# Down projection of a SwiGLU block: three of four quads in 32-row strips throughout

## The chip, the cores and the metric

The kernel runs on one core of one Trainium2 chip. TensorE does the matrix multiplications into eight PSUM banks, VectorE and ScalarE read the banks, SyncE issues most transfers. The metric is the device time of one execution in microseconds (us); the time of a version is the median of its runs. One execution is also profiled, and its span (from its first to its last instruction) is a little shorter than its time.

## What is computed

```
B, S, D, F = 1, 2048, 512, 1376
g = silu(x @ w_gate)
u = x @ w_up
out = (g * u) @ w_down
```

All inputs and the output are bf16. S is 2048 rows (tokens), D is 512, F is 1376, which is ten blocks of 128 and a remainder of 96.

## The kernel before

**Gate and up.** Tokens are split into four chunks of 512 columns (`SC`, `NSC`), each into four tiles of 128 tokens (`TPC`). For each chunk c and each of the ten whole blocks of F (`ft`), `plan_pair` plans a group G (gate) and a group U (up): four matmuls each over D, 512 columns wide. ScalarE applies silu to G, VectorE multiplies it with U and writes `hT_sb[:, ft, tokens]` (L280, L289). So `hT_sb` holds the hidden values with F on the partitions.

**The remainder of 96.** It is laid out in strips of 32 rows (`R`). Each chunk has an X group (`plan_x`): the last 96 gate columns and the last 32 up columns together. Two Y groups (`plan_y`) hold the other 64 up columns of two chunks each. VectorE's products of X and Y go to `ht_sb[32c:32c+32, q, :]`: chunk c lies on its own 32 partitions, with q = 0, 1, 2 (`NR`) counting the strips of the remainder. The two Y groups come last of all groups before the down projection. VectorE makes nine products of them: two for each chunk, and one for `hl_sb`, which the last output tile uses.

**Down projection.** There are 16 output tiles of 128 tokens x 512 columns. Each tile needs ten matmuls with 128 rows (`hT_sb` against `wd_sb`) and the remainder of 96 rows. Tiles are grouped into four quads: quad j holds tile j of each of the four chunks, so that the four tiles of a quad have their remainders on four different groups of 32 partitions. `whole_rows` (L394) does the ten 128-row matmuls of a tile. `tail_rows` (L408) does the remainder of a quad: three rounds (q) of four matmuls of 32 rows, each on another row group of TensorE's array, so that four can run side by side, and each into another bank.

The order is: quad 0 whole, quad 0 tail, quad 1 tail, quad 1 whole; then the same for quads 2 and 3. The last tile of quad 3 is split into columns 0 to 384 and 384 to 512; the narrow piece is the group `last`, and its remainder is one matmul with 96 rows (L431).

**Banks and waits.** Groups take the eight banks in turn (`add_group`), in the order in which they are planned: transposes, the four chunks with their X, the two Y, then the output groups in tile order. Thus a group's bank was last used by the group eight before it. `free(g)` makes TensorE wait until the readers of that earlier group are done. For quad 0 these are the eighth U group of the last chunk (counted from 1), the ninth G and U, and the tenth G; for quad 1 they are the last U, the last X and the two Y groups. `after` waits for a count on ScalarE's or VectorE's semaphore, and `need` for a load. TensorE's instructions run in program order.

**Copies and stores.** VectorE copies each finished output bank to one of three buffers `o_sb` (`NOS`; L293); ScalarE copies only the 384-wide piece of the last tile. SP issues the stores in tile order (L258), each after its copy, and waits at the end for all of them.

## Time and profile before

| what | us |
|---|---|
| median of 3 runs | 120.66 (120.31 to 120.93) |
| the profiled execution | 120.32 |
| its span | 118.9 |
| start of the down projection | 79.19 |
| first tail (quads 0 and 1), start | 87.93 |
| second tail (quads 2 and 3), start | 106.71 |
| last matmul, start | 116.78 |
| last store landed, end of the span | 118.9 |

Two more groups of the page, for later use (line, engine, operation, out<-in, shapes, count, then the busy time, the mean of one in ns, and the idle time of the engine before them with what ended it):

```profile
L394 PE MATMUL bank<-wd_sb,hT_sb 128*128 128x512 bf16 (+2 forms) x166 | 34.5, 366 | 0.4 <-issue 0.3
L293 DVE CAST o_sb<-bank 128x512 bf16<-128x512 f32 (+1 forms) x16 | 10.1, 663 | 22.0 <-PE bank L408 12.3
```

How to read them: PE is TensorE's matmuls, PEld its weight loads, DVE VectorE, ACT ScalarE, SP SyncE. Matmuls are pipelined: one of 379 ns starts before the one ahead of it has ended, so the pitch of starts and not the duration of one gives the rate. Some matmul records are missing from a trace: here about one in fifty, which is why 166 are listed where the program issues 170. In timelines the first column is the start in us and the second the time that the merged instructions cover.

### The profile page before, as it was taken

What the parts mean: (1) busy time and instruction counts of PE and PEld (TensorE: products, weight loads), DVE (VectorE), ACT (ScalarE), POOL (GpSimd) and SP (SyncE); (2) the same over time, 40 slices, a digit from 0 to 9 for tenths busy, and PEclk for the clock granted to TensorE, in tenths of its full rate; (3) what the DMA queues carried; (4) which work ended last, traced back from release to release, by engine and by line L of the source; (5) the groups of instructions that cost most, each with busy time, mean ns of one, the idle gap of its engine ahead of it and who ended that gap; (6) DMA issues with size and microseconds to landing.
All of it is one profiled execution on the core that took longest, in us unless ns stands there. A gap on an engine that the chain in (4) does not pass through costs nothing.

```text
span 118.9 us, 1519 instructions
## 1 busy us (share of the span) xinstructions
PE 115.4 (97%) x600; PEld 54.1 (45%) x611; DVE 47.3 (40%) x73; ACT 31.0 (26%) x53; POOL 0.4 (0%) x5
## 2 busy tenths in 40 slices
PE   7999999999999999999999999999999999999993
PEld 2774444444444444444444444344434444444452
DVE  0133443353443444433444334469617422006530
ACT  4344324454234363244262343230000000000001
POOL 1000000000000000000000000000000000000000
PEclk9999999999999999999999999999999999999999
DMA  3999999970000000000000000000004221002412
GB/s 103 271 307 357 264 162 242 328 183 24 0 0 0 6 0 0 0 3 3 0 0 0 6 0 0 0 0 0 0 0 138 88 88 44 0 0 75 145 50 88
DMA packets 17559, 8.84 MB, mean 74 GB/s; under 512 B 10640, under 2 KB 17424, under 8 KB 17552
## 3 DMA queue, kind: packets, MB, share of 16 engines
q1 hardware_dynamic: 16496, 8.48, 26.7%
q10 hardware_dynamic: 1056, 0.26, 1.0%
q8 instruction: 5, 0.08, 0.3%
q14 instruction: 2, 0.02, 0.1%
HBM read 4.81 MB, written 2.10 MB: 58 GB/s over the span
## 4 chain that ended last, share of the span: by engine, by line
PE 97%; issue 1%; DVE 0%
PE bank L328 58%; PE bank L394 29%; PE bank L370 3%; PE bank L337 2%; PE bank L408 2%; PE bank L381 2%; PE bank L346 1%; DVE o_sb L293 0%; PE bank L431 0%
## 5 line engine op out<-in xcount | busy, mean ns | idle before, releaser
L328 PE MATMUL bank<-xT_sb,w_sb 128*128 128x512 bf16 (+2 forms) x338 | 69.7, 364 | 0.4
L328 PEld LDWEIGHTS bank<-xT_sb,w_sb 128*128 128x128 bf16 x344 | 32.8, 98 | 36.4 <-issue 0.2
L289 DVE TENSOR_TENSOR hT_sb<-sg_sb,bank 128x512 bf16<-128x512 f32 x40 | 27.5, 688 | 40.5 <-PE bank L328 36.6
L394 PE MATMUL bank<-wd_sb,hT_sb 128*128 128x512 bf16 (+2 forms) x166 | 34.5, 366 | 0.4 <-issue 0.3
L280 ACT ACTIVATE sg_sb<-bank 128x512 f32<-128x512 f32 x40 | 23.8, 596 | 40.8 <-PE bank L328 40.8
L394 PEld LDWEIGHTS bank<-wd_sb,hT_sb 128*128 128x128 bf16 x170 | 16.1, 98 | 19.1 <-issue 1.3
L293 DVE CAST o_sb<-bank 128x512 bf16<-128x512 f32 (+1 forms) x16 | 10.1, 663 | 22.0 <-PE bank L408 12.3
L280 ACT ACTIVATE o_sb<-bank 128x384 bf16<-128x384 f32 x1 | 0.5, 492 | 37.8 <-PE bank L394 37.8
L289 DVE TENSOR_TENSOR ht_sb<-sgy_sb,bank 32x512 bf16<-32x512 f32 x8 | 5.5, 684 | 0.2
L289 DVE TENSOR_TENSOR ht_sb<-sgx_sb,bank 32x512 bf16<-32x512 f32 x4 | 2.8, 691 | 3.5 <-ACT sgx_sb L280 3.5
L370 PE MATMUL bank<-xT_sb,w_sb 128*128 128x512 bf16 x15 | 4.1, 379 | 0.1
L337 PE MATMUL bank<-const-bfloat16-1.0 128*128 128x512 bf16 (+1 forms) x8 | 2.9, 545 | 0.8 <-PEq L454 0.8
L280 ACT ACTIVATE sgx_sb<-bank 32x512 f32<-32x512 f32 x4 | 2.4, 588 | 4.5 <-PE bank L370 4.5
L408 PE MATMUL bank<-wdt_sb,ht_sb 32*128 32x512 bf16 (+1 forms) x48 | 2.9, 372 | 0.0
L370 PEld LDWEIGHTS bank<-xT_sb,w_sb 128*128 128x128 bf16 x16 | 1.6, 98 | 1.9
L280 ACT ACTIVATE sgy_sb<-bank 64x512 f32<-64x512 f32 x4 | 2.4, 590 | 0.1
L337 PEld LDWEIGHTS bank<-const-bfloat16-1.0 128*128 128x128 bf16 x8 | 1.0, 136 | 2.4 <-issue 2.4
L381 PE MATMUL bank<-xT_sb,w_sb 128*64 128x512 bf16 x16 | 1.9, 382 | 0.0
L408 PEld LDWEIGHTS bank<-wdt_sb,ht_sb 32*128 32x128 bf16 x48 | 1.1, 93 | 1.7 <-issue 0.8
L269 ACT ACT_TABLE_LOAD x1 | 1.3, 1283 | 1.8 <-issue 1.8
L293 DVE COPY xT_sb<-bank 128x256 bf16<-128x256 bf16 x2 | 0.6, 292 | 2.7 <-PE bank L346 2.7
L381 PEld LDWEIGHTS bank<-xT_sb,w_sb 128*64 128x64 bf16 x16 | 0.8, 109 | 1.0 <-DVE hT_sb L289 0.4
(14 smaller groups left out, 4.0 us busy)
## 6 DMA issues: line engine op xcount, KB each, us to landing
out_dram<-o_sb SPq DMA_DIRECT2D x15, 128.0 KB, 1.7
wd_sb<-in_w_down_dram SPq DMA_DIRECT2D x1, 1280.0 KB, 9.2
w_sb<-in_w_gate_dram SPq DMA_DIRECT2D x1, 480.0 KB, 5.9
w_sb<-in_w_up_dram SPq DMA_DIRECT2D x1, 448.0 KB, 6.5
w_sb<-in_w_gate_dram SPq DMA_DIRECT2D x1, 384.0 KB, 4.5
w_sb<-in_w_up_dram SPq DMA_DIRECT2D x1, 384.0 KB, 5.1
wdt_sb<-in_w_down_dram SPq DMA_DIRECT2D x4, 96.0 KB, 7.5
xn_sb<-in_x_dram SPq DMA_DIRECT2D x1, 256.0 KB, 2.8
```

The lines of the kernel that those rows point to most:

```text
L269: act.activation(adummy[:, 0:4], zero_c, ACT.Silu)
L280: act.activation(op["out"], op["src"], fn).then_inc(s_A, 1)
L289: ins = dve.tensor_tensor(op["out"], op["a"], op["b"], ALU.mult)
L293: ins = dve.tensor_copy(op["out"], op["src"])
L328: ins = pe.matmul(g["bank"][:, n0:n1], lhsT=w_sb[:, dk, col:col + P], rhs=xT_sb[:, dk, c * SC + n0:c * SC + n1], start=(dk == 0), stop=(dk ...
L337: pe.matmul(banks[NB - 1][:, 0:width], lhsT=ones_w, rhs=ones_m[:, 0:width], start=True, stop=True)
L346: ins = pe.transpose(tview(g["bank"])[:, k, :], xn_sb[:, g["i"], dk * P:(dk + 1) * P], ident[:, :])
L370: ins = pe.matmul(g["bank"][:, :], lhsT=w_sb[:, dk, XC0:XC0 + P], rhs=xT_sb[:, dk, c * SC:(c + 1) * SC], start=(dk == 0), stop=(dk == KD - 1),
L381: ins = pe.matmul(g["bank"][y0:y1, :], lhsT=w_sb[:, dk, YC0:YC0 + 64], rhs=xT_sb[:, dk, c * SC:(c + 1) * SC], start=(dk == 0), stop=(dk == ...
L394: ins = pe.matmul(g["bank"][:, 0:c1 - c0], lhsT=hT_sb[:, fk, t * P:(t + 1) * P], rhs=wd_sb[:, fk, c0:c1], start=(start and fk == 0), stop= ...
L408: ins = pe.matmul(g["bank"][:, 0:c1 - c0], lhsT=ht_sb[R * c:R * (c + 1), q, j * P:(j + 1) * P], rhs=wdt_sb[R * c:R * (c + 1), q, c0:c1], s ...
```

## The change

Quads 0, 1 and 2 (`qa`, `qb`, `qc`) are computed in strips of 32 rows: `whole_rows` remains for quad 3 (`qd`) and for the narrow piece of the last tile. A 128-row block of F is cut into four strips of 32 rows. In a round, the four tiles of a quad each run one strip of the same block, tile c on row group (c - turn) mod 4; after ten rounds (one per block of F) the turn goes up by one, so that after four turns each tile has had all four strips. [...]

The order is: ten rounds of `qa`, ten of `qb`, alternating through turns 0, 1, 2; turn 3 of `qa`; both tails (three rounds each); turn 3 of `qb`. Then `qc`: its tail and turn 0 (13 rounds), and before each of its turns 1, 2, 3 one round of `qd`'s tail. Then `qd` whole, and the narrow piece.

There are eight output buffers instead of three, and in the first three quads ScalarE makes the copies of the tiles with odd c.

```diff
-    NOS = 3
+    NOS = 8
...
-                eng = "A" if len(halves) == 2 and c0 == 0 else "D"
+                eng = "A" if (j < TPC - 1 and c % 2) or (len(halves) == 2 and c0 == 0) else "D"
...
-            for i in range(NOS):
-                sp.wait_ge(s_out[i], 16 * n_store[i])
+            for i in range(NST, NST + NOS):
+                sp.wait_ge(s_out[i % NOS], 16 * n_store[i % NOS])
...
             def whole_rows(g, start, stop):
-                free(g)
-                after("D", h_ready[g["c"]])
+                if start:
+                    free(g)
...
+            def strips(quad, pieces, start, stop):
+                nonlocal n_turn
+                last_turn, mark = turned.get(id(quad), (None, 0))
+                if last_turn not in (None, pieces[0][0]):
+                    pe.wait_ge(s_T, mark)
+                for n, (turn, h, w) in enumerate(pieces):
+                    for c, g in enumerate(quad):
+                        r = (c - turn) % NSC
+                        if start and n == 0:
+                            free(g)
+                        c0, c1 = g["c0"], g["c1"]
+                        ins = pe.matmul(
+                            g["bank"][:, 0:c1 - c0], lhsT=h(r, g["t"]), rhs=w[R * r:R * (r + 1), c0:c1],
+                            start=(start and n == 0), stop=(stop and n == len(pieces) - 1),
+                            tile_position=(R * r, 0), skip_group_check=True,
+                        )
+                        if stop and n == len(pieces) - 1:
+                            ins.then_inc(s_P, 1)
+                if not stop:
+                    n_turn += 1
+                    ins.then_inc(s_T, 1)
+                turned[id(quad)] = (pieces[-1][0], n_turn)
+
+            def body(turn):
+                return [
+                    (turn, lambda r, t, fk=fk: hT_sb[R * r:R * (r + 1), fk, t * P:(t + 1) * P], wd_sb[:, fk, :])
+                    for fk in range(NFF)
+                ]
+
+            def tail(qs):
+                return [
+                    (0, lambda r, t, q=q: ht_sb[R * r:R * (r + 1), q, (t % TPC) * P:(t % TPC + 1) * P], wdt_sb[:, q, :])
+                    for q in qs
+                ]
...
+            strips(qa, body(0), True, False)
+            strips(qb, body(0), True, False)
+            strips(qa, body(1), False, False)
+            strips(qb, body(1), False, False)
+            strips(qa, body(2), False, False)
+            strips(qb, body(2), False, False)
+            strips(qa, body(3), False, False)
+            for c in range(NSC):
+                need(f"wdt{c}")
+            after("D", max(t_ready.values()))
+            strips(qb, tail(range(NR)), False, False)
+            strips(qa, tail(range(NR)), False, True)
+            strips(qb, body(3), False, True)
+            strips(qc, tail(range(NR)) + body(0), True, False)
+            for turn in range(1, NSC):
+                strips(qd, tail([turn - 1]), turn == 1, False)
+                strips(qc, body(turn), False, turn == NSC - 1)
+            for g in qd:
+                whole_rows(g, False, True).then_inc(s_P, 1)
             whole_rows(last, True, False)
```

More of the change, by code (lines that the diff above doesn't have):

```diff
@@ L73, in bass_standalone__swiglu_ffn__prompt_kernel @@
         s_D = sem("s_D")
+        s_T = sem("s_T")
         s_out = [sem(f"s_out{i}") for i in range(NOS)]
@@ L399, in whole_rows @@
                 return ins
-            def tail_rows(quad, start, stop):
-                for q in range(NR):
-                    for g in quad:
-                        if q == 0:
+            turned = {}
+            n_turn = 0
+            def strips(quad, pieces, start, stop):
[7 more added lines that the diff above has]
+                        if start and n == 0:
@@ L405, in tail_rows @@
                             free(g)
-                        c, c0, c1 = g["c"], g["c0"], g["c1"]
-                        j = g["t"] % TPC
+                        c0, c1 = g["c0"], g["c1"]
                         ins = pe.matmul(
-                            g["bank"][:, 0:c1 - c0], lhsT=ht_sb[R * c:R * (c + 1), q, j * P:(j + 1) * P],
-                            rhs=wdt_sb[R * c:R * (c + 1), q, c0:c1],
-                            start=(start and q == 0), stop=(stop and q == NR - 1),
-                            tile_position=(R * c, 0), skip_group_check=True,
+                            g["bank"][:, 0:c1 - c0], lhsT=h(r, g["t"]), rhs=w[R * r:R * (r + 1), c0:c1],
+                            start=(start and n == 0), stop=(stop and n == len(pieces) - 1),
+                            tile_position=(R * r, 0), skip_group_check=True,
@@ L413, in tail_rows @@
                         )
-                        if stop and q == NR - 1:
+                        if stop and n == len(pieces) - 1:
                             ins.then_inc(s_P, 1)
-            need("wd")
-            for j in range(0, TPC, 2):
-                for g in quads[j]:
-                    whole_rows(g, True, False)
-                for c in range(NSC):
-                    need(f"wdt{c}")
-                after("D", max(t_ready.values()))
-                tail_rows(quads[j], False, True)
-                tail_rows(quads[j + 1], True, False)
-                for g in quads[j + 1]:
-                    whole_rows(g, False, True).then_inc(s_P, 1)
+                if not stop:
+                    n_turn += 1
+                    ins.then_inc(s_T, 1)
@@ new lines, in on_tensor @@
+            qa, qb, qc, qd = quads
+            need("wd")
+            for c in range(NSC):
+                after("D", h_ready[c])
+            strips(qa, body(0), True, False)
[5 more added lines that the diff above has]
+            strips(qa, body(3), False, False)
+            for c in range(NSC):
+                need(f"wdt{c}")
```

## The prediction

> **What bounds the kernel now.** I read four views in this order: the page's busy table and chain of waits, its costliest groups, the timeline around the down projection, and narrow timelines for single starts.

> ```profile
> PE 115.4 (97%) x600; PEld 54.1 (45%) x611; DVE 47.3 (40%) x73; ACT 31.0 (26%) x53; POOL 0.4 (0%) x5
> ...
> PE 97%; issue 1%; DVE 0%
> PE bank L328 58%; PE bank L394 29%; PE bank L370 3%; PE bank L337 2%; PE bank L408 2%; PE bank L381 2%; PE bank L346 1%; DVE o_sb L293 0%; PE bank L431 0%
> ...
> L408 PE MATMUL bank<-wdt_sb,ht_sb 32*128 32x512 bf16 (+1 forms) x48 | 2.9, 372 | 0.0
> ```

> TensorE is the bound from end to end: 97% of the chain is its own matmuls, so a nanosecond added to its queue from 79 us on is a nanosecond of the end, and other engines matter only where TensorE waits for them. The L408 row shows that the existing 32-row tails already run four abreast: 48 matmuls of 372 ns need 2.9 us, not 17.9.

> The timeline from the last gate/up matmul on:

> ```profile
> 78.88 0.38 PE L381 MATMUL bank<-xT_sb,w_sb 128*64 128x512 bf16 x2
> 79.19 4.25 DVE L289 TENSOR_TENSOR ht_sb<-sgy_sb,bank 32x512 bf16<-32x512 f32 x6
> 79.19 6.43 PE L394 MATMUL bank<-wd_sb,hT_sb 128*128 128x512 bf16 x28
> 83.47 0.29 DVE L289 TENSOR_TENSOR hl_sb<-sgy_sb,bank 64x128 bf16<-64x128 f32 x1
> 83.79 1.41 DVE L289 TENSOR_TENSOR ht_sb<-sgy_sb,bank 32x512 bf16<-32x512 f32 x2
> ```

> While TensorE starts the down projection at 79.19, VectorE still forms the nine Y products (L289), the last until 83.79 + 1.41 = 85.20. They read the PSUM banks of the two Y groups, and those banks are the ones that the third and fourth tile of the second quad will write. Today TensorE touches the second quad only in its tail, after 87.93, so this work is hidden with 2.7 us to spare.

> **The clock of the rounds.** Single starts around the first tail:

> ```profile
> 87.19 0.81 PE L394 MATMUL bank<-wd_sb,hT_sb 128*128 128x512 bf16 x3
> 87.93 0.61 PE L408 MATMUL bank<-wdt_sb,ht_sb 32*128 32x512 bf16 x8
> 88.16 0.38 PE L408 MATMUL bank<-wdt_sb,ht_sb 32*128 32x512 bf16 x4
> 89.02 0.38 PE L408 MATMUL bank<-wdt_sb,ht_sb 32*128 32x512 bf16 x4
> 89.33 0.11 PEld L394 LDWEIGHTS bank<-wd_sb,hT_sb 128*128 128x128 bf16 x2 [0.42 <-issue]
> 89.56 17.21 PE L394 MATMUL bank<-wd_sb,hT_sb 128*128 128x512 bf16 x78 [0.16 <-issue]
> ```

> Rounds two to six of the tail start from 88.16 to 89.02: (89.02 - 88.16) / 4 = 0.215 us for four 32-row matmuls. A whole matmul has the same pitch: the three from 87.19 begin (87.19 + 0.81 - 0.38 - 87.19) / 2 = 0.215 apart. So a round of strips does the multiplications of one whole matmul in the time of one whole matmul, and splitting ten whole matmuls of four tiles (40) into 40 rounds of strips costs, by pitch, nothing: 120 rounds x (0.215 - 0.215). I take 0, with 0.3 us either way for the rounding of the two readings (120 x 0.0025).

> **The change, part by part.**

> 1. Switches between whole and strip matmuls. The last whole matmul starts at 87.62 (87.19 + 0.43), the first two rounds at 87.93 and 88.16: 0.54 us for two pitches of 0.215, so a switch costs 0.11. Leaving the tail: 89.02 to 89.56 is again 0.54 (two loads at 89.33 and 78 of 80 matmuls in the row say that the first whole matmul's record is missing), another 0.11. From the Y matmuls on, before has five switches (into L394, then in and out of two tails); after has two (into the strips, out of them before the fourth quad). Gain 3 x 0.11 = 0.33.

> 2. The wait that moves. Today the quads' banks are asked for tile by tile, and the second quad's at about 88.6. After the change, ten rounds of the first quad are followed at once by ten rounds of the second, and its first round asks for its four banks. Those are the banks of the last up group, the last X group and the two Y groups (a tile takes the bank of the group eight before it). First round at 79.19, tenth end at 79.19 + 10 x 0.215 + 0.01 = 81.35: the first two strips go; the third waits for four Y products (79.19 + 4 x 0.71 = 82.03), the fourth for all nine, 85.20. From a product's end to the load that waited for it the trace has 0.07 (the product that ends at 76.59 + 0.69 = 77.28, the L381 load at 77.34), and a separate wait instruction, where one is made, adds up to 0.1. So the round that was due at 81.35 runs at 85.27 to 85.35: **+3.9 to +4.0 us, 3.95**. Behind the waiting instruction stands everything TensorE has left, since its queue is in order; nothing that it could do meanwhile is ahead of it. VectorE's chain doesn't shorten: its products run back to back from 78.14 and depend on no strip. What is late next is all of the down projection, by the same 3.95, for no later stage has slack on TensorE.

> 3. The turns. When a quad's strips turn by a tile, another row group writes the same bank, so TensorE waits for its own previous block (the new semaphore). With ten or three rounds of another quad between (2.15 or 0.65 us) against 0.38 for a matmul's end plus 0.07, the wait is over before it is reached. For the third quad only one round of the fourth lies between, three times. The block's last strip starts at T, ends at T + 0.38, its successor can load at T + 0.45 and was due at T + 0.43. Lower end 0.02 each; upper end, if its weights (93 ns, the L408 load row) come after the wait and the wait is a separate instruction, 0.2. I take 0.1, the middle and near the 0.11 of a switch, which is also a load that could not be made ahead: 3 x 0.1 = 0.3, ends 0.06 and 0.6.

> 4. Half of the first three quads' copies go to ScalarE, and there are eight output buffers instead of three. VectorE's 1.4 us of waiting for output transfers and its 0.69 us copies lie beside TensorE. Their cover: a quad's banks are wanted again at least ten rounds (2.15 us) after it finishes, and two copies per engine (2 x 0.69; on ScalarE some 0.6 each, an estimate between the 492 ns of its 384-wide copy and the 596 ns of its 512-wide activation) take 1.4. Without the split, 4 x 0.69 = 2.8 would exceed the cover by 0.6; with it the cost is 0. The fifteen stores that SP issues are the same in number, size and order, and the fourth quad with its last copies and stores is as before: from the last matmul to the end stays about 2.1 us (116.78 to 118.9). Five more final waits on SP, some 0.02 each as the ones now, lie under the last store's landing: 0.

> 5. Some 360 more matmuls and 360 more loads. The pitch above counts them if TensorE is fed in time; see the third rival.

> Sum: 3.95 - 0.33 + 0.3 = **+3.9 us**. On the profiled execution, 120.32 us (span 118.9 and 1.4 around it), that is 124.2; on the median of the three runs, 120.66, 124.6. I forecast 124.4; its own range, with the bounds above and the runs' spread of 0.6, is 123.7 to 125.2.

> **Rivals.**

> *The clock falls in the gap.* At the start TensorE runs at half speed:

> ```profile
> 1.58 0.15 PEld L337 LDWEIGHTS bank<-const-bfloat16-1.0 128*128 128x128 bf16 x1 [0.28 <-issue]
> 2.01 0.15 PEld L337 LDWEIGHTS bank<-const-bfloat16-1.0 128*128 128x128 bf16 x1 [0.28 <-issue]
> 2.44 0.15 PEld L337 LDWEIGHTS bank<-const-bfloat16-1.0 128*128 128x128 bf16 x1 [0.28 <-issue]
> ```

> A 512-wide matmul each 0.43 us, twice 0.215 (the granted-clock row reads 9 there all the same), until about 4.1, 3.3 us after its first matmul. In the new gap TensorE does one strip round's third member at 82.1 and is otherwise idle from 81.75 to 85.3. If that is enough to slow it again, the next 2.6 to 3.3 us run at half speed: +1.3 to +1.65, 125.7 to 126.1. For it: the gap is as long as that warm-up. Against: the strip in it, and no gap of before (the longest on TensorE is under 0.8) shows what is tolerated. 0.22. [...]

> *Feeding.* A round is eight instructions in 0.215 us, 27 ns each, for 132 rounds; before it never lasted beyond 48 instructions, which could be queued ahead. The nearest long row is narrow pairs just after a wait:

> ```profile
> 4.65 0.94 PEld L328 LDWEIGHTS bank<-xT_sb,w_sb 128*128 128x128 bf16 x16
> ```

> (0.94 - 0.10) / 15 = 56 ns a pair, which is also what a 128-wide matmul needs, so it only says that a pair takes at most 56. At 56 a round takes 0.224: 132 x 0.009 = +1.2, 125.6. 0.06. [...]

> *The wait is not there.* If the second quad's banks were free by 81.4, only parts 1 and 3 would remain: -0.33 + 0.3, or -0.27 at best: 120.1 to 120.3, not slower. It decides at the last Y product: 85.20 would have to be before 81.4, and neither the products nor the bank order change. 0.04. That the strips run but serially (no overlap) falls by the L408 row.

> **How the numbers follow.** Forecast 0.66, clock 0.22, feeding 0.06, no wait 0.04; 0.02 stays for turns beyond their bound. The range 123.7 to 126.2 takes in the forecast, the clock case and the feeding case at 56 ns. A measurement of this kernel can tell about 0.5% (0.6 us) from no change: faster by more 0.02, within 0.03, slower 0.95.

> **What would show it.** Right: a hole of some 3.5 us on TensorE from 81.7 with one strip in it, released by L289's last Y product at 85.2; rounds of 0.215 before and after; three small gaps of about 0.1 in the third quad; the fourth quad starting some 3.9 late. The clock rival shows as rounds of 0.43 after the hole, the feeding rival as rounds over 0.22 all through. I am wrong if TensorE has no hole near 82, or if rounds differ from 0.215.

## The result and the profile after

The median is 125.67 us, against 120.73 for the kernel before in the same six rounds; the ratio is 1.037 with a 95% interval of 1.033 to 1.041. This ratio and those below leave out runs over 1.5% above the kernel's fastest, here the 127.42, so they can differ from the ratio of the medians. The profiled execution takes 125.67 us with a span of 124.4, 5.4 more than the span before (unrounded, 124.35 against 118.92). The six executions are not one heap: 124.14 and 124.31 have a mean granted clock of 1.000, 125.67 (twice) and 125.85 have 0.986, 127.42 has 0.973.

Of the page of the changed kernel, the lines that answer to those of before (the chain by engine and by line, then the rows of strips, which now have line L416):

```profile
PE 117.7 (95%) x963; PEld 56.7 (46%) x971; DVE 43.3 (35%) x67; ACT 34.2 (28%) x59; POOL 0.4 (0%) x5
...
PEclk9999999999999999999999999997799999999999
...
PE 91%; issue 3%; DVE 3%; ACT 1%; DVEq 0%
PE bank L329 56%; PE bank L416 23%; PE bank L395 7%; PE bank L371 3%; DVE ht_sb L290 2%; PE bank L338 2%; ACT sgy_sb L281 0%; ACT sgx_sb L281 0%; DVE hl_sb L290 0%; DVE xT_sb L294 0%; DVE o_sb L294 0%; PE bank L347 0%; PE bank L466 0%; DVEq L289 0%
...
L416 PE MATMUL bank<-wd_sb,hT_sb 32*128 32x512 bf16 x480 | 29.7, 391 | 3.2 <-DVE ht_sb L290 3.2
```

TensorE has lost the chain for a while: VectorE's product line L290, which was not in the chain before, holds 2%, and some of the "issue" goes with it, since the chain now runs through ScalarE and VectorE until 85.3. The granted clock has a dent, 7 in two of the 40 slices. And 480 strips of 391 ns, 188 us in a row, take 29.7 us of the engine: four lie side by side, and a round starts before the one ahead of it has ended.

The timeline of the changed kernel from the first strip on, with rows left out at the dots (start, time covered, engine, line, count, and the wait before it):

```profile
79.16 4.25 DVE L290 TENSOR_TENSOR ht_sb<-sgy_sb,bank 32x512 bf16<-32x512 f32 x6
79.16 2.55 PE L416 MATMUL bank<-wd_sb,hT_sb 32*128 32x512 bf16 x42
82.10 0.09 PEld L416 LDWEIGHTS bank<-wd_sb,hT_sb 32*128 32x128 bf16 x1 [0.89 <-DVE ht_sb L290]
82.13 0.37 PE L416 MATMUL bank<-wd_sb,hT_sb 32*128 32x512 bf16 x1 [0.42 <-DVE ht_sb L290]
83.44 0.29 DVE L290 TENSOR_TENSOR hl_sb<-sgy_sb,bank 64x128 bf16<-64x128 f32 x1
83.76 1.41 DVE L290 TENSOR_TENSOR ht_sb<-sgy_sb,bank 32x512 bf16<-32x512 f32 x2
85.28 0.15 PEld L416 LDWEIGHTS bank<-wd_sb,hT_sb 32*128 32x128 bf16 x8 [3.10 <-DVE ht_sb L290]
85.32 10.04 PE L416 MATMUL bank<-wd_sb,hT_sb 32*128 32x512 bf16 x149 [2.82 <-DVE ht_sb L290]
...
86.07 0.20 PEld L416 LDWEIGHTS bank<-wd_sb,hT_sb 32*128 32x128 bf16 x4 [0.23 <-issue]
86.50 0.20 PEld L416 LDWEIGHTS bank<-wd_sb,hT_sb 32*128 32x128 bf16 x4 [0.23 <-issue]
```

Ten rounds (40 strips) and two strips of the eleventh run from 79.16; the third strip waits for the fourth Y product and runs at 82.13, the fourth waits for the last (83.76 + 1.41 = 85.17) and runs at 85.3. After that the loads come every 0.43 us, twice the pitch. The same stretch by windows (length; busy us and count of PE, PEld, DVE, ACT, POOL; then the granted clock, DMA share and GB/s), cut at the two times at which the clock changed, 85.41 and 88.82, and one such length before and after:

```profile
81.99:85.41 3.42, 0.47 (x5) 0.22 (x9) 3.03 (x5) 0.00 (x0) 0.00 (x0) 1.00 0.00 0
85.41:88.82 3.41, 3.41 (x36) 1.62 (x38) 0.00 (x0) 0.00 (x0) 0.00 (x0) 0.50 0.02 5
88.82:92.23 3.41, 3.41 (x72) 1.85 (x65) 0.00 (x0) 0.00 (x0) 0.00 (x0) 1.00 0.00 0
```

The clock is halved for exactly one stretch of 3.41 us, just as the work comes back: 36 strips are at work in it, 72 in the next.

### The profile page after: what moved, and what is told of

The parts are those of the page before. It is cut to its first block, busy times and chain, and to the rows that moved or that the text cites. A ratio compares the mean times of both kernels' runs of the same rounds, so it can differ in the third digit from the quotient of the medians.

```text
span 124.4 us, 2243 instructions
## 1 busy us (share of the span) xinstructions
PE 117.7 (95%) x963; PEld 56.7 (46%) x971; DVE 43.3 (35%) x67; ACT 34.2 (28%) x59; POOL 0.4 (0%) x5
## 4 chain that ended last, share of the span: by engine, by line
PE 91%; issue 3%; DVE 3%; ACT 1%; DVEq 0%
PE bank L329 56%; PE bank L416 23%; PE bank L395 7%; PE bank L371 3%; DVE ht_sb L290 2%; PE bank L338 2%; ACT sgy_sb L281 0%; ACT sgx_sb L281 0%; DVE hl_sb L290 0%; DVE xT_sb L294 0%; DVE o_sb L294 0%; PE bank L347 0%; PE bank L466 0%; DVEq L289 0%
## 5 line engine op out<-in xcount | busy, mean ns | idle before, releaser
L290 DVE TENSOR_TENSOR hT_sb<-sg_sb,bank 128x512 bf16<-128x512 f32 x40 | 27.5, 687 | 40.7 <-PE bank L329 36.6
L416 PE MATMUL bank<-wd_sb,hT_sb 32*128 32x512 bf16 x480 | 29.7, 391 | 3.2 <-DVE ht_sb L290 3.2
L416 PEld LDWEIGHTS bank<-wd_sb,hT_sb 32*128 32x128 bf16 x480 | 14.2, 96 | 17.7 <-DVE ht_sb L290 4.0
L294 DVE CAST o_sb<-bank 128x512 bf16<-128x512 f32 (+1 forms) x10 | 6.2, 648 | 31.3 <-PE bank L416 25.9
L281 ACT ACTIVATE o_sb<-bank 128x512 bf16<-128x512 f32 (+1 forms) x7 | 3.7, 580 | 40.0 <-PE bank L416 32.9
L395 PE MATMUL bank<-wd_sb,hT_sb 128*128 128x512 bf16 (+2 forms) x49 | 8.6, 336 | 0.2 <-issue 0.2
L395 PEld LDWEIGHTS bank<-wd_sb,hT_sb 128*128 128x128 bf16 x50 | 4.5, 98 | 4.6 <-issue 0.4
L290 DVE TENSOR_TENSOR ht_sb<-sgy_sb,bank 32x512 bf16<-32x512 f32 x8 | 5.5, 684 | 0.2
L290 DVE TENSOR_TENSOR ht_sb<-sgx_sb,bank 32x512 bf16<-32x512 f32 x4 | 2.8, 692 | 3.5 <-ACT sgx_sb L281 3.5
L416 PE MATMUL bank<-wdt_sb,ht_sb 32*128 32x512 bf16 (+1 forms) x48 | 3.9, 371 | 0.0
L416 PEld LDWEIGHTS bank<-wdt_sb,ht_sb 32*128 32x128 bf16 x48 | 1.6, 93 | 1.2
```

Of the source, the lines that this page charges most:

```text
L281: act.activation(op["out"], op["src"], fn).then_inc(s_A, 1)
L290: ins = dve.tensor_tensor(op["out"], op["a"], op["b"], ALU.mult)
L294: ins = dve.tensor_copy(op["out"], op["src"])
L395: ins = pe.matmul(g["bank"][:, 0:c1 - c0], lhsT=hT_sb[:, fk, t * P:(t + 1) * P], rhs=wd_sb[:, fk, c0:c1], start=(start and fk == 0), stop= ...
L416: ins = pe.matmul(g["bank"][:, 0:c1 - c0], lhsT=h(r, g["t"]), rhs=w[R * r:R * (r + 1), c0:c1], start=(start and n == 0), stop=(stop and n ...
```

## The experiments

Seven kernels ran. "Held" below means a mean granted clock of 1.000, and "fell" a lower one; a kernel's time is set against the kernel before on the same chip (120.50 for the first four, 120.53 for the last three).

**Quad 0 whole again, quads 1 and 2 in strips.** The changed kernel's order of strips is replaced; nothing else.

```diff
-            strips(qa, body(0), True, False)
-            strips(qb, body(0), True, False)
...
-            strips(qa, body(3), False, False)
+            for g in qa:
+                whole_rows(g, True, False)
             for c in range(NSC):
                 need(f"wdt{c}")
             after("D", max(t_ready.values()))
-            strips(qb, tail(range(NR)), False, False)
             strips(qa, tail(range(NR)), False, True)
-            strips(qb, body(3), False, True)
+            strips(qb, tail(range(NR)) + body(0), True, False)
             strips(qc, tail(range(NR)) + body(0), True, False)
             for turn in range(1, NSC):
-                strips(qd, tail([turn - 1]), turn == 1, False)
+                strips(qb, body(turn), False, turn == NSC - 1)
                 strips(qc, body(turn), False, turn == NSC - 1)
+            strips(qd, tail(range(NR)), True, False)
```

> Quad 0 goes back to whole matmuls, only quads 1 and 2 run in strips, so the second quad's banks are first wanted at about 88.5 us, after the last Y product (85.2). Theory (the loss is the moved wait plus the clock it lets fall): no hole near 82, no slow rounds, three switches between whole and strips instead of five, 120.7 - 2 x 0.11 = 120.5 us, granted clock 1.000 in every run. Rival (480 short matmuls cost by themselves, by feeding or by the turns): two thirds of the strips remain, so some two thirds of the loss should remain, 123 us or more.

Measured: 120.22 us, ratio 0.9978 (0.9963 to 0.9992), held in all twelve executions. From its chain of work (start, us, what):

```profile
77.52 1.85 PE bank L382 x16
79.36 8.74 PE bank L395 x40
88.10 19.96 PE bank L416 x365
108.07 8.77 PE bank L395 x50
```

No step of another engine stands in it. From the start of the first matmul of the down projection to that of the last it is 116.67 - 79.30 = 37.37 us; before, 116.78 - 79.19 = 37.59. The difference is the 0.22 of two saved switches. With 320 strips of the 480 left, the rival is out: short matmuls side by side, their turns with ten rounds between included, cost nothing that shows here. This version is 0.2% faster than the kernel before, the only one here that beats it.

**The hole filled with idle work.** Sixteen matmuls of ones whose result is overwritten.

```diff
             strips(qa, body(0), True, False)
+            free(qb[0])
+            for i in range(16):
+                pe.matmul(qb[0]["bank"][:, :], lhsT=ones_w, rhs=ones_m, start=True, stop=True)
             strips(qb, body(0), True, False)
```

> The changed kernel, with sixteen 512-wide matmuls of ones put into the hole (into the first bank of the second quad, before its strips overwrite it); the wait for the last Y product stays as long. Theory: the hole's length costs 3.9 us and the fall of the clock is a separate 1.3 to 1.7 on top, which busy matmuls prevent: every run has a granted clock of 1.000 and they lie together at 124.2 us (124.0 to 124.6). Rival (the clock falls for another cause, such as the strips' own load): falls and runs at 125.7 stay, in about as many executions.

Measured: 124.70 us (124.03 to 124.99), ratio 1.034 (1.031 to 1.037), held in all six. Its timeline:

```profile
81.75 3.67 PE L447 MATMUL bank<-const-bfloat16-1.0 128*128 128x512 bf16 x16
...
84.08 1.41 DVE L290 TENSOR_TENSOR ht_sb<-sgy_sb,bank 32x512 bf16<-32x512 f32 x2
85.36 0.10 PEld L416 LDWEIGHTS bank<-wd_sb,hT_sb 32*128 32x128 bf16 x3 [0.42 <-issue]
85.36 6.93 PE L416 MATMUL bank<-wd_sb,hT_sb 32*128 32x512 bf16 x123
```

TensorE's strips come as late as in the changed kernel, but it is busy until then, and 123 strips lie within 6.93 us: the full pitch, at once. So the slow rounds come from the emptiness of the hole, not from the strips. The median is 0.5 us above the expected 124.2 and just outside the expected 124.0 to 124.6. In the profiled execution the way from the first strip to the last matmul is 3.75 us longer than from the same place in the kernel before (41.34 against 37.59), as the hole, the turns and the saved switches should make it (3.76, below); it reaches its first strip 0.29 us later (79.48 against 79.19), in a part that no edit touches, and the executions of the kernels here scatter by as much.

**The wait alone, in the kernel before.**

```diff
-                for g in quads[j]:
+                for n, g in enumerate(quads[j]):
+                    if n == 1:
+                        after("D", max(t_ready.values()))
                     whole_rows(g, True, False)
```

> The kernel before with nothing changed but the wait for the last Y product, moved ahead of the second tile's whole matmuls (at 81.35 us instead of 87.9). Theory: the moved wait alone makes the loss: a hole from 81.7 to 85.3, +3.9 us where the clock holds (124.6) and +5.2 to +5.6 where it falls (126.0 to 126.3); as nothing at all runs in this hole, the clock falls at least as often as in the changed kernel. Rival (the strips make part of the loss): less than +3.5 us where the clock holds.

Measured: one execution held, 124.35, which is +3.85; three have 0.986, 125.88 to 125.92; one has 0.973, 127.95; a sixth took 316 us at a clock of 1.000, from a cause that no view shows, and is left out. The ratio is 1.041 (1.037 to 1.046). From the first to the last matmul of the down projection the execution that held takes 41.49 us, 3.90 more than before. Its profile by windows in whole steps of 3.413 us from the rise of the clock at 5.04, which the trace records (in the changed kernel the clock fell 81.92 us after its rise, 24 such steps):

```profile
80.13:83.54 3.41, 1.59 (x8) 0.51 (x6) 3.29 (x5) 0.00 (x0) 0.00 (x0) 1.00 0.00 0
83.54:86.95 3.41, 1.50 (x7) 0.70 (x8) 1.76 (x4) 0.00 (x0) 0.00 (x0) 1.00 0.00 0
```

One moved wait, without a single added strip, copies the result of the change, all three of its heaps. In this execution the hole of 3.9 us was shared between two windows, with 47% and 44% of work, and the clock stayed at 1.00.

**Copies and buffers alone, in the kernel before.** `NOS = 8`, the odd tiles' copies on ScalarE, the last waits reordered.

> The kernel before with eight output buffers, the odd tiles' copies on ScalarE and the new order of the last waits, nothing else. Theory: none of it lies on the path, 120.7 us, the same within 0.3. Rival: the copies or the five more final waits take or give something at the end, 0.3 us or more, which would have to show between the last matmul and the end of the span (2.1 us in the kernel before).

Measured: 120.51 us, ratio 1.0004 (0.998 to 1.003). From the first to the last matmul of the down projection it takes 117.60 - 80.01 = 37.59 us, as before. No effect on the path, as expected.

**All three quads in strips, the second one late.**

```diff
             strips(qa, body(0), True, False)
-            strips(qb, body(0), True, False)
             strips(qa, body(1), False, False)
-            strips(qb, body(1), False, False)
             strips(qa, body(2), False, False)
+            strips(qb, body(0), True, False)
...
```

After that the quads alternate again, so that between two turns of a quad two or more rounds of another lie, but for the last turn of the third quad, which has one.

> Three quads in strips as in the changed kernel, but the first quad runs three turns of ten rounds before the second quad starts (at about 85.7 us, after the last Y product at 85.2), so the hole is gone and two of the first quad's turns follow each other with no round of another quad between. Theory: the strips as such gain 3 x 0.11 = 0.33 us for the saved switches, and each of the two bare turns costs one matmul's way to its end, some 0.25 us (next round at 0.46 instead of 0.216 after the last): 120.5 - 0.33 + 2 x 0.25 + a few hundredths = 120.7 us, granted clock 1.000 throughout. Rival (a bare turn is as cheap as the shadowed ones, below 0.05): 120.2.

Measured: 120.91 us, ratio 1.003 (1.001 to 1.005), held in all twelve. Two turns of its first quad, in narrow timelines of TensorE (`s_T` is counted up at the end of each block of rounds, and TensorE waits for it before the same quad goes on with another turn):

```profile
81.72 0.85 PE L416 MATMUL bank<-wd_sb,hT_sb 32*128 32x512 bf16 x8
82.18 0.40 PE L416 MATMUL bank<-wd_sb,hT_sb 32*128 32x512 bf16 x4
```

Eight strips are the last round of one turn, at 81.72, and the first of the next, at 82.18: 0.46 us instead of 0.216, 0.24 for a bare turn. Two of these eat the gain of the saved switches (2 x 0.24 - 0.33 = +0.15); from the first to the last matmul of the down projection it is 117.59 - 79.77 = 37.82 us, 0.23 more than before. The rival of cheap turns is out. The change's interleaving of quads is thus worth something; only its start was too early.

**Holes of other lengths, in the kernel before.** The same wait ahead of the sixteenth whole matmul of the first quad; in a second kernel ahead of the sixth, with 5 in place of 15.

```diff
+            n_whole = [0]
+
...
                 for fk in range(NFF):
+                    if n_whole[0] == 15:
+                        after("D", max(t_ready.values()))
+                    n_whole[0] += 1
```

> The kernel before with the wait for the last Y product ahead of the sixteenth whole matmul: a hole of 2.8 us. Theory (the clock falls only where a fixed window of 3.41 us is nearly empty of matmuls, under some 10 to 20%): the least busy window holds 0.6 us of matmuls, 18%, so no fall or nearly none, and the time is 120.5 + 2.8 = 123.3 us in one cluster. Rival (a window that is less than about a third busy is enough): some two in five executions fall and lie 1.2 to 1.7 above the others.

Measured: five of six executions held, 123.39 to 124.00; one fell, 124.99. Ratio 1.028 (1.025 to 1.032). The one that fell is the profiled one, by windows:

```profile
83.10:86.51 3.41, 1.02 (x5) 0.50 (x6) 2.24 (x4) 0.00 (x0) 0.00 (x0) 1.00 0.00 0
86.51:89.93 3.42, 3.42 (x10) 1.22 (x8) 0.00 (x0) 0.00 (x0) 0.00 (x0) 0.50 0.00 0
```

A window with 1.02 of 3.41 us of work, 30%, was followed by a slow one. The theory as I wrote it (a window nearly empty, under 10 to 20%) is wrong; the count alone, one of six, does not decide, but this row does. From the first to the last matmul of the down projection this execution is 4.51 us longer than before (42.10 against 37.59): 2.8 for the hole and 1.7 for the slow window.

> The kernel before with the wait ahead of the sixth whole matmul: a hole of 5.0 us. Both readings have the clock fall in most executions: a window of 3.41 us lies wholly inside the hole in (5.0 - 3.4) / 3.4 = 47% of the alignments, and one that is up to a third busy in all of them. Empty-window reading: about half of the executions at 120.5 + 5.0 = 125.5 us, half at 126.7 to 127.2. Third-busy reading: all of them above 126.5.

Measured: 127.84 to 128.35 in all four executions, each with 0.973; ratio 1.063 (1.061 to 1.064). By windows:

```profile
79.80:83.21 3.41, 0.99 (x5) 0.26 (x3) 3.25 (x6) 0.00 (x0) 0.00 (x0) 1.00 0.00 0
83.21:86.62 3.41, 1.01 (x3) 0.44 (x4) 2.24 (x4) 0.00 (x0) 0.00 (x0) 0.50 0.00 0
86.62:90.04 3.42, 3.20 (x9) 1.22 (x8) 0.00 (x0) 0.00 (x0) 0.00 (x0) 0.50 0.00 0
90.04:93.45 3.41, 3.41 (x17) 1.51 (x16) 0.00 (x0) 0.00 (x0) 0.00 (x0) 1.00 0.00 0
```

None held, as the third-busy reading has it. The first window, with 29% of work, was followed by half clock; so was the next, in which work is back for the last 1.0 us; after the third, with 3.20 of 3.42 us of work, the clock was 1.00. So this hole costs two slow windows, of which work lies in 4.4 us: from the first to the last matmul of the down projection it is 7.16 us longer than before (44.75 against 37.59), 5.0 for the hole and half of the 4.4.

## Why the prediction came out as it did

The direction and the place were right. The forecast of 124.4 is 1.3 below the median, and it was the likeliest case that was chosen wrongly: the median is that of the clock rival. The range holds the median only because it had been stretched to take in the rivals; the forecast's own range ended at 125.2.

- *What bounds the kernel*: right. TensorE waits for VectorE only in the hole, and everything after it is late by the hole.
- *Part 1, switches*: right. Five became two; the version with three gained the 0.22 that two of them cost.
- *Part 2, the moved wait, 3.95 us*: right. The eleventh round's fourth strip was due with its second, which started at 79.16 + 2.55 - 0.37 = 81.34; it ran at 85.32, 3.98 late; the wait alone in the kernel before cost 3.85, or 3.90 by its trace. The load that waited came 0.11 after the product's end (85.28 against 85.17); the 0.1 for a separate wait on top of the 0.07 was an estimate, and such an instruction takes 0.051 us on TensorE in the trace of before (L308, eight of them).
- *Part 3, the turns, 0.3 us*: mis-sized. The third quad's turns have one round between. The second of them puts its round at 0.46 instead of 0.43 after the block's last one:

```profile
108.38 0.38 PE L416 MATMUL bank<-wd_sb,hT_sb 32*128 32x512 bf16 x4
108.60 0.38 PE L416 MATMUL bank<-wdt_sb,ht_sb 32*128 32x384 bf16 x4
108.84 0.40 PE L416 MATMUL bank<-wd_sb,hT_sb 32*128 32x512 bf16 x4
```

With the 0.01 by which the round behind is late, three such turns cost some 0.1, near the lower end of 0.06. I had priced them like a switch (0.11 each); one with a round between costs about a third of that.

- *Part 4, copies and buffers*: right, 0 (ratio 1.0004). Whether the split was needed for that, no run shows.
- *Part 5 and the feeding rival*: strips keep a pitch of 0.216 a round wherever the clock is full. The rival is out: a pair of strip and load took 0.216 / 4 = 54 ns here, for over a thousand instructions, less than the 56 of its price. That the 48 instructions of before could be queued ahead was a supposition; no run tests it.
- *The clock rival, 0.22*: this is the step that failed. Its price, 1.3 to 1.65, was near, though no row that it showed gave the lower end (2.6 us of slow work, as the six 512-wide matmuls of the start would take at 0.43 each): nine pitches after the hole cover 85.32 to 88.94, 3.62 us instead of 1.94, so +1.68. Its chance was too low, because I took the strip at 82.1, and the lack of a gap in the kernel before that shows what is tolerated, as reasons against it. Four of six executions fell, and of the wait alone four of five. The window before the fall held 0.47 us of work, 14%; in the holes of other lengths the clock fell after 29% and 30% too, and in the wait's execution that held it stayed after 44%. With a limit between these, some 55% (at 30%) to 82% (at 44%) of the alignments of a 3.41 us grid with this hole fall; this is an estimate from the two idle pieces of the hole, 81.71 to 82.13 and 82.50 to 85.32.

The sum with what was measured: 3.98 for the hole, 1.68 for the clock, 0.1 for the turns, less 0.32 for three switches, +5.44; the spans differ by 5.4, and so does the way from the first to the last matmul of the down projection (43.03 against 37.59). For the two executions that held, 124.14 and 124.31, the first, third and fourth terms alone give 3.76, on 120.73 some 124.5; they lie 0.2 to 0.35 below that, within the spread of the kernel before (120.31 to 120.93).

What stays open is the share of work below which the clock falls, if a share decides; the rows here put it between 30% and 44% by the profile's busy time, which is modelled at the ends of matmuls, if the window that decides is the one that ends where the clock changes; no run tests that apart. The 2.8 us hole speaks for the lower end: by the same estimate it would fall in some 44% of alignments at a limit of 30% and 72% at 44%, and one of six fell. Open too is what it takes to lift a low clock (30% did not, 94% did), and why one execution each of the change and of the moved wait, 127.42 and 127.95, has 0.973, the mean clock that the 5.0 us hole has with two slow windows; no profile of these was kept.

## What to carry to other kernels

When an order of tiles is changed, list for each tile who last used its bank and when that reader ends; an accumulation that starts early takes its bank early, even where its data come late (here a round ran 3.98 us late for it). A hole on TensorE can have two prices, its length and a stretch at half clock after it, and the second comes and goes between executions (here in one of six after a hole of 2.8 us, in eight of eleven after 3.6 to 3.9, in all four after 5.0); a heap of times with a second heap some 1.5 us above it, and the granted clock in the windows behind the hole, give it away. Splitting 128-row matmuls of four tiles into 32-row strips on four banks was free in time here (0.216 us a round against 0.215 a matmul), so it can be used to avoid changes of the array's shape (0.11 us each), if at least one round of another quad lies between two turns of a bank (0.03 us for a turn then, 0.24 without).
